# Gate sums with sixteen consecutive tokens in a partition, and gate rows written in 64-byte pieces

## Chip, core and metric

The kernel runs on one core of one Trainium2 chip. The metric is the device time of one execution in microseconds (us). Three runs of the kernel before took 879.82, 880.47 and 882.48 us; the median is 880.47.

The engines are called TensorE (PE in the profile; its weight loads are PEld), VectorE (DVE), ScalarE (ACT), GpSimd (POOL) and SyncE (SP). SBUF is the on-chip memory with 128 partitions, PSUM holds the eight banks into which TensorE accumulates, and DRAM is the memory off the core that only DMAs reach. A DMA is issued by one of the engines, here nearly always SP for loads and POOL for intermediate stores, and is carried out by 16 DMA engines.

## What is computed

The input x has 2048 tokens of 640 features. Two branches read it and a gate mixes them:

```python
x = A_x
g = _sigmoid((x * gate_w).sum(-1, keepdims=True))
a = _A_ref(x, A_dft_seq_re, A_dft_seq_im, A_dft_hid_re, A_dft_hid_im)
b = _B_ref(x, B_w1, B_b1, B_w2)
return g * a + (1 - g) * b
```

Branch A is the real part of a Fourier transform over features and tokens, written as matrix products: `y = Cr @ (x @ Wr^T) - Ci @ (x @ Wi^T)`. Branch B is a dense layer of 1728 units, the Mish activation, and a dense layer back to 640. The gate g is one number for each token: the sigmoid of the sum over features of x times `gate_w`.

## The kernel before

All products are float32 in accuracy, made on TensorE from a high and a low part. For each operand ScalarE rounds the tile to a high part (a tile `r3h` or `w14h`), VectorE subtracts it from the tile to get the low part (`r3l`, `w14l`), and three matmuls (high x high, high x low, low x high) go into the same PSUM bank. There are ten pairs of moving operands r0 to r9 of 128 x 512, so ScalarE and VectorE can run ten operands ahead of TensorE. The larger products use a scheme with seven in place of eight block products, for which VectorE adds and subtracts tiles beforehand (line 259) and adds results afterwards.

Tokens are cut into four groups t of 512. The work runs in this order:

1. Four sequence problems `sq[0]` to `sq[3]` (real and imaginary part, two pairs of token groups each): the sequence DFT matrices against x. Their results u go through DRAM (`u<-f` stores by POOL, `f<-u` loads by SP).
2. Two hidden problems `hd[0]` and `hd[1]` (two token groups each): the hidden DFT matrices against u. Their results are multiplied by g, token by token, and stored as y in DRAM.
3. The first dense layer, with Mish, and for token groups 2 and 3 a product with 1 - g; results go to DRAM as act.
4. Two output problems `ou[0]` and `ou[1]`: the second dense layer, with y added, to the output.

Each of these problems has three parts, `first`, `second` and `third`. The end of `third` reads the PSUM banks out (`done`, `give`, lines 499 to 515); with `self.q` set, as for the hidden problems, the reading is a VectorE product with a tile that holds g of the token group in all 128 partitions. The `second` of the next problem starts accumulating into the same banks.

The order of instructions is decided while the kernel is built. Everything is recorded in a graph of operations with their dependencies, and `Graph.run` (lines 99 to 184) is a list scheduler with a modelled cost for each operation. The order in which it picks operations is the order of each engine's program. The modelled size that it gets for the gates' row writes is a constant, `1 << 18`. Besides waiting for what they read or overwrite, SP's DMAs go round eight semaphores: each waits for the one issued eight earlier to land. A wait at the head of an engine's program holds everything behind it on that engine.

The gate is made by `gates()`, which is recorded between the second and third part of `sq[2]`:

- `gate_w` is loaded into all 128 partitions (`wide`).
- For each k from 0 to 15 a tile of 128 tokens is loaded into an x buffer (line 745), and VectorE multiplies it with `wide` and sums over the features into column k of `gcol`, a tile of 128 x 16 (line 746). In x as the kernel holds it, [16, 128, 640], tile k has tokens 128 k to 128 k + 127, so that `gcol[p, k]` belongs to token 128 k + p.
- ScalarE takes the sigmoid of `gcol` (line 750), VectorE makes `qcol` = 1 - `gcol` (line 751).
- Both are written to DRAM rows `grow` and `qrow` of 2048 numbers in the order of tokens (line 753). In this order element (p, k) goes to place 128 k + p.
- Later, `broadcast` (line 542) loads 512 numbers of a row into all 128 partitions as one tile f. `grow` is used by the hidden problems, `qrow` by the first dense layer and `ou[0]`.

Of the kernel before, what the change touches and what calls it, by code (L numbers as in the profile page):

```python
# [14 lines left out]
S, D, F = 2048, 640, 1728  # L15
P = 128
N = 512
TG = S // N
KS = S // P
# [173 lines left out]
def fnet_mish_gate(ctx: ExitStack, tc: tile.TileContext, xn, xt, c_re, c_im, wd_re, wd_im,  # L193
                   w1a, w1b, b1a, b1b, w2, gw, out):
    nc = tc.nc
# [11 lines left out]
    X = Pool("x", [sb.tile([P, D], F32, name=f"x{i}") for i in range(NX)], FS, lambda t: t[:, :N])  # L207
# [20 lines left out]
    def whole(*vals):  # L228
        return [(v, None) for v in vals]

    def dve(emit, r, w, n=N, more=0.0):
        took = 0.15 + n / 960 + more
        return G.add("DVE", emit, r, w, took, took - 0.083)

    def act(emit, r, w, n=N, more=0.0):
        took = 0.21 + n / 1260 + more
        return G.add("ACT", emit, r, w, took, took - 0.096)

    def dma(queue, emit, r, w, size):
        return G.add(queue, emit, r, w, 1.95 + size / 385e3, 0.605 if queue == "SP" else 1.0)  # L240
# [3 lines left out]
    def load(pool, src, of=None, rows=P, cols=N, queue="SP"):  # L244
        v = Val(pool)
        dma(queue, lambda: ISSUE[queue].dma_start(v.t[:rows, :cols], src() if callable(src) else src),
            whole(of) if of else [], whole(v), rows * cols * 4)
        return v
# [492 lines left out]
    def gates():  # L741

        wide = load(X, gw.partition_broadcast(P), cols=D)
        for k in range(KS):
            x = load(X, xn[k], cols=D)
            dve(lambda k=k, x=x: nc.vector.scalar_tensor_tensor(  # L746
                x.t, x.t, 1.0, wide.t, op0=OP.mult, op1=OP.mult, accum_out=gcol.t[:, k:k + 1]),
                whole(x, wide), whole(x) + [(gcol, k)], D, 0.1)
        cols = [(gcol, k) for k in range(KS)]
        act(lambda: nc.scalar.activation(gcol.t, gcol.t, AF.Sigmoid), cols, cols, KS)  # L750
        dve(lambda: nc.vector.tensor_scalar(qcol.t, gcol.t, -1.0, 1.0, op0=OP.mult, op1=OP.add), cols, whole(qcol), KS)
        for c, row, r in ((gcol, grow, cols), (qcol, qrow, whole(qcol))):
            dma("SP", lambda c=c, row=row: nc.sync.dma_start(row.t.rearrange("o (k p) -> p (o k)", p=P), c.t),
                r, whole(row), 1 << 18)
        act(lambda: nc.scalar.preload_act_table_set("mish"), cols, whole(table), 0, 1.0)

# [29 lines left out]
    for q in range(4):  # L786
        if q == 3:
            sq[3].first(seq_top)
        sq[q].second(seq.low)
        if q == 2:  # L790
            gates()
        sq[q].third()
# [64 lines left out]
```

## Time and profile before

| What | Before |
|---|---|
| Median of three runs | 880.47 us (879.82 to 882.48) |
| Profiled execution, its time | 882.19 us |
| Profiled execution, its span | 880.4 us |
| Instructions | 11973 |
| DMA traffic | 203.50 MB, mean 231 GB/s |
| Mean granted TensorE clock | 0.994 |

The span is the time from the first to the last instruction of the core; the time of the execution has some 1.8 us around it. In the profile a row of a timeline gives the start, the duration in us, the engine, the line of the kernel, the operation and the tiles as `out<-in`, with buffer numbers left out (`f<-u` is any load of a u tile into any f buffer), and in square brackets the idle time of the engine just before and what ended it. A row of waits gives the engine, line and tile that waited, what it waited for, the total in us, how often, and the longest. A row of a table of stretches gives the stretch (start:end in us), its length, and for PE, PEld, DVE, ACT and POOL the busy time with the count of instructions, then the granted TensorE clock, the DMA engines' mean busy share and the GB/s that they moved. A row of DMA issues gives the transfer, the issuing engine, the count, the size, and the median time in us from issue to landing. The chain of waits gives the start, the duration and what the end of the work waited for in that time.

### The profile page before, as it was taken

How to read it: one execution, taken by the hardware profiler on the slowest of the kernel's cores; microseconds unless marked ns; L12 is line 12 of the kernel's file. 1: busy time of each engine (PE TensorE's matmuls, PEld its weight loads, DVE VectorE, ACT ScalarE, POOL GpSimd, SP SyncE). 2: the span in 40 equal slices, each digit the busy share in tenths (PEclk: the TensorE clock that was granted, in tenths of full speed). 3: DMA queues.
4: the chain of work that ended last, by engine and by line, in shares of the span. 5: the costliest groups of instructions: out<-in, count | busy, mean ns of one | idle time of the engine just before them, and what ended most of it. 6: DMA issues, size and time to landing. Idle time of an engine off the chain costs nothing.

```text
span 880.4 us, 11973 instructions
## 1 busy us (share of the span) xinstructions
PE 861.5 (98%) x3772; PEld 710.2 (81%) x3772; DVE 677.8 (77%) x1213; ACT 461.6 (52%) x849; POOL 69.3 (8%) x132
## 2 busy tenths in 40 slices
PE   9999999999999999999995999999999999999998
PEld 7888888888888888888884888888888888887786
DVE  7899957866785667997976999924666997739891
ACT  7675535535453445674552576745655755522541
POOL 0000001002000200011001102111111100000000
PEclk9999999999999999999997999999999999999999
DMA  9796939555954755559975959565444687526943
GB/s 319 273 337 223 324 123 366 181 204 164 346 191 146 254 202 179 196 200 367 374 193 154 373 179 338 211 222 190 146 159 188 214 304 265 199 77 221 366 160 119
DMA packets 107071, 203.50 MB, mean 231 GB/s; under 512 B 16640, under 2 KB 19072, under 8 KB 107008
## 3 DMA queue, kind: packets, MB, share of 16 engines
q1 hardware_dynamic: 96752, 169.57, 56.5%
q0 software_dynamic: 10112, 33.04, 10.0%
q8 instruction: 29, 0.48, 0.2%
q14 instruction: 34, 0.28, 0.1%
q10 hardware_dynamic: 144, 0.13, 0.0%
HBM read 164.40 MB, written 38.29 MB: 230 GB/s over the span
## 4 chain that ended last, share of the span: by engine, by line
PE 85%; DMA 6%; DVE 6%; ACT 1%; issue 1%; SPq 0%; ACTq 0%; DVEq 0%
PE ps L292 85%; DMA f<-u 4%; DVE f L259 3%; DMA x<-in_xn_dram 1%; DMA f<-po 1%; DVE x L746 1%; DVE x L259 0%; DVE r8l L287 0%; ACT f L268 0%; DVE r9l L287 0%; DMA out_dram<-f 0%; ACT r8h L286 0%; DVE r1l L287 0%; DVE r5l L287 0%; ACT r1h L286 0%
## 5 line engine op out<-in xcount | busy, mean ns | idle before, releaser
L259 DVE TENSOR_TENSOR f<-f,f 128x512 f32<-128x512 f32 x316 | 211.8, 686 | 19.6 <-DMA f<-u 15.3
L268 ACT ACTIVATE f<-ps 128x512 f32<-128x512 f32 x129 | 74.5, 595 | 40.2 <-PE ps L292 35.1
L259 DVE TENSOR_TENSOR f<-ps,f 128x512 f32<-128x512 f32 x92 | 59.8, 684 | 38.4 <-PE ps L292 38.3
L255 POOL DMA_DIRECT2D u<-f x40 | 21.5, 540 | 321.6 <-DVE f L259 310.3
L286 ACT ACTIVATE r4h<-f 128x512 fp32r<-128x512 f32 x40 | 25.2, 629 | 37.9 <-PE ps L292 20.2
L286 ACT ACTIVATE r6h<-f 128x512 fp32r<-128x512 f32 x40 | 25.3, 631 | 37.5 <-PE ps L292 17.3
L286 ACT ACTIVATE r1h<-f 128x512 fp32r<-128x512 f32 x39 | 24.5, 629 | 33.0 <-PE ps L292 17.7
L550 ACT ACTIVATE f<-f,b1s 128x512 f32<-128x512 f32 x36 | 25.6, 722 | 28.2 <-DVE f L259 28.1
L286 ACT ACTIVATE r3h<-f 128x512 fp32r<-128x512 f32 x41 | 25.8, 629 | 26.0 <-PE ps L292 13.1
L286 ACT ACTIVATE r2h<-f 128x512 fp32r<-128x512 f32 x41 | 25.8, 628 | 25.4 <-PE ps L292 16.6
L286 ACT ACTIVATE r9h<-f 128x512 fp32r<-128x512 f32 x42 | 26.4, 629 | 23.1 <-PE ps L292 10.7
L255 POOL DMA_DIRECT2D act<-f x52 | 28.2, 542 | 131.0 <-DVE f L259 65.3
L286 ACT ACTIVATE r5h<-f 128x512 fp32r<-128x512 f32 x40 | 25.1, 629 | 25.3 <-PE ps L292 13.3
L287 DVE TENSOR_TENSOR r3l<-f,r3h 128x512 fp32r<-128x512 f32 x41 | 28.2, 688 | 11.6 <-ACT r3h L286 11.2
L286 ACT ACTIVATE r8h<-f 128x512 fp32r<-128x512 f32 x39 | 24.5, 629 | 24.0 <-PE ps L292 14.8
L286 ACT ACTIVATE r0h<-f 128x512 fp32r<-128x512 f32 x40 | 25.1, 629 | 22.1 <-PE ps L292 13.9
L287 DVE TENSOR_TENSOR r9l<-f,r9h 128x512 fp32r<-128x512 f32 x42 | 28.9, 688 | 9.6 <-ACT r9h L286 9.0
L287 DVE TENSOR_TENSOR r0l<-f,r0h 128x512 fp32r<-128x512 f32 x40 | 27.5, 688 | 11.4 <-ACT r0h L286 11.3
L287 DVE TENSOR_TENSOR r2l<-f,r2h 128x512 fp32r<-128x512 f32 x41 | 28.2, 688 | 10.0 <-ACT r2h L286 9.7
L287 DVE TENSOR_TENSOR r8l<-f,r8h 128x512 fp32r<-128x512 f32 x39 | 26.8, 688 | 11.3 <-ACT r8h L286 11.0
L287 DVE TENSOR_TENSOR r6l<-f,r6h 128x512 fp32r<-128x512 f32 x40 | 27.5, 688 | 9.7 <-ACT r6h L286 9.4
L287 DVE TENSOR_TENSOR r5l<-f,r5h 128x512 fp32r<-128x512 f32 x40 | 27.5, 688 | 9.2 <-ACT r5h L286 8.9
(1827 smaller groups left out, 2650.0 us busy)
## 6 DMA issues: line engine op xcount, KB each, us to landing
f<-in_c_re_dram SPq DMA_DIRECT2D x128, 256.0 KB, 4.9
f<-in_c_im_dram SPq DMA_DIRECT2D x128, 256.0 KB, 3.5
f<-act SPq DMA_DIRECT2D x84, 256.0 KB, 5.2
f<-u SPq DMA_DIRECT2D x80, 256.0 KB, 5.7
act<-f POOLq DMA_DIRECT2D x52, 256.0 KB, 2.9
f<-in_xt_dram SPq DMA_DIRECT2D x44, 256.0 KB, 4.4
u<-f POOLq DMA_DIRECT2D x40, 256.0 KB, 5.2
x<-in_xn_dram SPq DMA_DIRECT2D x25, 320.0 KB, 5.7
```

Of the source, the lines that this page charges most:

```text
L255: dma(queue, lambda: ISSUE[queue].dma_start(d.t, v.t[:rows]), whole(v), whole(d), rows * N * 4)
L259: dve(lambda: nc.vector.tensor_tensor(o.t[rows, x], a.t[rows, y], b.t[rows, z], op=op), whole(a, b), whole(o), n)
L268: act(lambda: nc.scalar.activation(o.t, a.t, AF.Copy, scale=scale), whole(a), whole(o))
L286: act(lambda: nc.scalar.activation(r.t[0][:, :N], src.t[:, :N], AF.Copy), whole(src), [(r, 0)])
L287: dve(lambda: nc.vector.tensor_tensor(r.t[1][:, :N], src.t[:, :N], f32(r.t[0][:, :N]), op=OP.subtract), whole(src) + [(r, 0)], [(r, 1)])
L292: G.add("PE", lambda: nc.tensor.matmul(bank.t, w.t[wn][:, k * P:k * P + P], x.t[xn_][:, :N], start, stop, skip_group_check=True), [(w, (k, ...
L550: act(lambda: nc.scalar.activation(o.t[rows], src.t[rows], AF.Mish, **more), whole(src, table) + whole(b1s) * bias, whole(o), more=0.1)
L746: dve(lambda k=k, x=x: nc.vector.scalar_tensor_tensor(x.t, x.t, 1.0, wide.t, op0=OP.mult, op1=OP.mult, accum_out=gcol.t[:, k:k + 1]), whol ...
```

## The change

```diff
     def gates():
 
         wide = load(X, gw.partition_broadcast(P), cols=D)
+        tokens = xn.rearrange("k p d -> (k p) d").rearrange("(p k) d -> k p d", k=KS)
         for k in range(KS):
-            x = load(X, xn[k], cols=D)
+            x = load(X, tokens[k], cols=D)
             dve(lambda k=k, x=x: nc.vector.scalar_tensor_tensor(
                 x.t, x.t, 1.0, wide.t, op0=OP.mult, op1=OP.mult, accum_out=gcol.t[:, k:k + 1]),
                 whole(x, wide), whole(x) + [(gcol, k)], D, 0.1)
...
         for c, row, r in ((gcol, grow, cols), (qcol, qrow, whole(qcol))):
-            dma("SP", lambda c=c, row=row: nc.sync.dma_start(row.t.rearrange("o (k p) -> p (o k)", p=P), c.t),
+            dma("SP", lambda c=c, row=row: nc.sync.dma_start(row.t.rearrange("o (p k) -> p (o k)", k=KS), c.t),
                 r, whole(row), 1 << 18)
```

Tile k of the gate's loads now has the tokens k, 16 + k, 32 + k and so on, one for each partition: a partition's row is still 640 numbers (2560 bytes) in one piece, and the rows of neighbouring partitions are 16 tokens, 40,960 bytes, apart in DRAM, where they were 2560 bytes apart. `gcol[p, k]` then belongs to token 16 p + k, so that the 16 numbers of a partition are 16 neighbours in the row. The row writes, 8 KB each, put each partition's 64 bytes at one place; before, each of the 2048 numbers of 4 bytes went to a place of its own. The contents of `grow` and `qrow` and all that reads them are the same. The sizes, the dependencies and the modelled costs that the scheduler sees are the same as well, and so is the order of each engine's program.

## The prediction

> **What bounds the kernel now.** I read five views in this order: the totals by engine, TensorE's waits over the whole span, the chain of waits from 440 us on, sums of short stretches with the DMA rate, and the timelines of the engines around the one large gap. TensorE is busy nearly all the span, and more than half of what it lacks is a single wait:
>
> ```profile
> PE 861.5 (98%) x3772; PEld 710.2 (81%) x3772; DVE 677.8 (77%) x1213; ACT 461.6 (52%) x849; POOL 69.3 (8%) x132
> ```
> ```profile
> PE ps L292 <- DVE f L259: 10.3, 1, 10.3
> PE ps L292 <- ACT ps L268: 2.2, 3, 1.5
> ```
> ```profile
> 469.91 0.39 PE L292 MATMUL ps<-r3l,w15h 128*128 128x512 f32 x1
> 470.13 0.39 PE L292 MATMUL ps<-r3h,w15l 128*128 128x512 f32 x1
> 480.82 0.76 PE L292 MATMUL ps<-r4h,w11h 128*128 128x512 f32 x1 [10.30 <-DVE f L259]
> ...
> 484.77 0.39 PE L292 MATMUL ps<-r5h,w21h 128*128 128x512 f32 x1
> ```
>
> The pace is one matmul in 0.227 us (469.91 to 470.13, and 133 recorded in 30 us further below). So the matmul at 480.82 was due at 470.36, and the one at 484.77, nine matmuls on, at 470.36 + 9 x 0.227 = 472.40. TensorE has lost 12.4 us by then: 10.46 of standing still, and 1.9 because the nine ran at half clock (the first row of the next fence, granted clock 0.50). This is the seam between the first and second hidden-DFT problem, and the wait is on VectorE reading a PSUM bank that the next problem overwrites. Why is VectorE late? The stretches show the DMA rate, in the last column, almost vanish twice; the last but one is the DMA share:
>
> ```profile
> 474.50:484.70 10.20, 3.88 (x9) 3.13 (x10) 10.02 (x17) 4.62 (x8) 3.40 (x7) 0.50 0.46 160
> ...
> 400.00:430.00 30.00, 30.00 (x133) 24.78 (x132) 25.00 (x50) 13.34 (x25) 2.53 (x5) 1.00 1.04 390
> 430.00:442.00 12.00, 12.00 (x54) 9.95 (x53) 12.00 (x23) 6.66 (x13) 0.00 (x0) 1.00 1.01 371
> 447.00:454.00 7.00, 7.00 (x32) 5.82 (x31) 3.61 (x6) 3.50 (x6) 0.00 (x0) 1.00 0.42 34
> 462.50:469.00 6.50, 6.50 (x30) 5.38 (x29) 1.19 (x2) 0.63 (x1) 0.00 (x0) 1.00 0.46 31
> 445.00:474.50 29.50, 25.52 (x113) 20.82 (x111) 16.56 (x32) 7.92 (x14) 0.00 (x0) 1.00 0.67 143
> ```
> ```profile
> 442.10 0.37 SPq L753 DMA_DIRECT2D grow<-gcol  x1
> ```
> ```profile
> 442.77 12.22 DMA f<-u
> ...
> 457.44 0.37 SPq L753
> ...
> 457.86 13.29 DMA f<-u
> ```
> ```profile
> f<-u SPq DMA_DIRECT2D x80, 256.0 KB, 5.7
> grow<-gcol SPq DMA_DIRECT2D x1, 8.0 KB, 11.9
> qrow<-qcol SPq DMA_DIRECT2D x1, 8.0 KB, 11.1
> ```
>
> Each hole follows one of the two row writes, issued at 442.1 and 457.44. An 8 KB write takes 11.9 and 11.1 us to land, and the 256 KB load issued right behind it 12.2 and 13.3 instead of the usual 5.7. For 7 and 6.5 us the queues hold work (DMA share 0.42 and 0.46) and move 34 and 31 GB/s, where 390 is normal. In the program a row write is 2048 pieces of 4 bytes: consecutive tokens lie in different partitions, so no two elements of a partition are neighbours in the row. VectorE then stands waiting for loads:
>
> ```profile
> 447.43 0.69 DVE L287 TENSOR_TENSOR r7l<-f,r7h 128x512 fp32r<-128x512 f32 x1
> 450.38 0.69 DVE L259 TENSOR_TENSOR f<-f,f 128x512 f32<-128x512 f32 x1 [2.27 <-DMA f<-u]
> ...
> 455.02 0.69 DVE L259 TENSOR_TENSOR f<-f,f 128x512 f32<-128x512 f32 x1 [2.14 <-DMA f<-u]
> ...
> 467.81 0.69 DVE L259 TENSOR_TENSOR f<-f,f 128x512 f32<-128x512 f32 x1 [7.07 <-DMA f<-u]
> ...
> 471.24 0.69 DVE L259 TENSOR_TENSOR f<-f,f 128x512 f32<-128x512 f32 x1 [1.47 <-DMA f<-u]
> ...
> 476.40 3.08 DVE L259 TENSOR_TENSOR f<-ps,f 128x512 f32<-128x512 f32 x5
> ...
> 479.99 1.28 DVE L259 TENSOR_TENSOR f<-ps,f 128x512 f32<-128x512 f32 x2
> ...
> 483.59 1.28 DVE L259 TENSOR_TENSOR f<-ps,f 128x512 f32<-128x512 f32 x2
> 484.79 0.68 DVE L287 TENSOR_TENSOR r9l<-f,r9h 128x512 fp32r<-128x512 f32 x1
> ```
>
> The four waits are 12.95 us. The bank reads at 476.40 to 483.59 stand behind them in VectorE's order, and the first of the pair at 479.99 frees the bank that TensorE waits for.
>
> **The change, part by part.** The order of instructions on every engine is the same in both kernels, so no queue is reshuffled and no instruction added. Three things differ.
>
> *The row writes.* Each becomes 128 pieces of 64 bytes, one for each partition, in place of 2048. No small write to DRAM other than these two stands in this trace. Bounds of a landing: the ordinary 5.7 us of a load in a full queue (or the 4.6 of a store, below) from one side, the 11.9 of today from the other. If the holes go with the number of pieces, 7 and 6.5 us become 7/16 = 0.44 and 6.5/16 = 0.41; if with the bytes, nothing changes. I take the first: the DMA engines had the same work queued in the holes as before them, and ordinary stores, with 32 times the bytes in long pieces, land in 4.6 us.
>
> The Trainium skill (DMA: Bandwidth & Descriptors, Specifications) speaks against half of this: a transfer below 512 bytes costs a read-modify-write, and 64 is still below. If each piece pays, the holes shrink by 16 as above; if being small were enough to stop the queue, the time would stay.
>
> *What becomes of the stall.* VectorE from 448.1 to 484.79 has 36.7 - 12.95 = 23.7 us of work, so without waits it could start r9l at 471.8. Its bank reads must also wait for TensorE. By the program's order the last 30 matmuls before the seam are 18 for one group of banks and 12 for the last pair, so the banks come free at 470.36 - 30 x 0.227 = 463.6, at 467.6 and at 470.4. VectorE would reach the five reads of 476.40 at 476.4 - 12.95 = 463.5, just when the first banks are done; the read that releases TensorE (479.99, now 467.0 at the earliest) waits for 467.6 and ends by 468.3, 2 us before TensorE needs it at 470.36. The last pair starts at 470.4, so r9l starts at about 471.8, 13 us earlier than 484.79. TensorE thus loses neither the 10.46 nor the 1.9 us.
>
> Can the DMAs keep up? From 445 to 474.5 they moved 29.5 us x 143 GB/s = 4.2 MB; at 385 GB/s that is 11 us, so it can be in by 456 to 460 even where SP issues late. The next loads hang on the stores of y, which follow the products with g:
>
> ```profile
> 480.04 1.60 POOL L255 DMA_DIRECT2D y<-f  x3 [58.42 <-DVE f L259]
> ```
> ```profile
> 483.30 20.59 SPq L246 DMA_DIRECT2D f<-u  x25
> ```
> ```profile
> y<-f POOLq DMA_DIRECT2D x20, 256.0 KB, 4.6
> x<-in_xn_dram SPq DMA_DIRECT2D x25, 320.0 KB, 5.7
> ```
>
> The first store waits for a product after the five bank reads: 463.6 + 5 x 0.6 + 0.6 = 467.2 in place of 480.04, so the 25 loads that begin at 483.30 begin 12 to 13 us earlier too. The whole pipeline moves, not TensorE alone. That matters, because VectorE is then full for long, and TensorE gets an operand only just in time:
>
> ```profile
> 496.00:575.00 79.00, 79.00 (x350) 65.45 (x349) 78.75 (x156) 54.72 (x112) 10.87 (x20) 1.00 0.74 261
> ```
> ```profile
> 552.12 0.68 DVE L287 TENSOR_TENSOR r5l<-f,r5h 128x512 fp32r<-128x512 f32 x1
> ```
> ```profile
> 553.72 0.39 PE L292 MATMUL ps<-r5l,w17h 128*128 128x512 f32 x1
> ```
>
> VectorE is busy 78.75 of 79 us here, and r5l is ready at 552.80, 0.9 us before use. If VectorE came only 10 us earlier, TensorE would stall 12.4 - 10 - 0.9 = 1.5 us.
>
> *The token loads.* The 16 loads of x for the gates take rows 16 apart, a pitch of 40,960 bytes instead of 2560, still 128 pieces of 2560 bytes. They lie in 400 to 442 us, where the DMAs are full, but TensorE has a cushion there:
>
> ```profile
> 423.42 0.68 DVE L287 TENSOR_TENSOR r3l<-f,r3h 128x512 fp32r<-128x512 f32 x1
> ```
> ```profile
> 433.87 0.39 PE L292 MATMUL ps<-r3l,w0h 128*128 128x512 f32 x1
> ```
>
> r3l waits 433.87 - 424.10 = 9.8 us for its use. No load with this pitch stands in the trace. Bounds: no extra, or each 320 KB (0.84 us at 390 GB/s) at half speed, 16 x 0.84 = 13.4 us, of which the cushion takes 9.8 and 3.6 us would show. I take nothing, since the pieces keep their size.
>
> The Trainium skill (DMA: Bandwidth & Descriptors, Latency and other measured facts) lists copies that lose from a 2 MiB row pitch on, and full speed at 512 KiB; 40 KiB is far below, and by it the sum stays. No run shows it yet.
>
> **Sum.** 10.46 + 1.9 = 12.4 us off the profiled execution's 882.19 us (880.4 of span and 1.8 around it) is 869.8. That execution lies 1.7 above the median of 880.47. If the 1.7 lies elsewhere the changed median is 868.1; if the stall itself varies between runs it goes with it, and 869.8 holds for all. I take 868.9, a gain of 11.6.
>
> **The rivals.**
> - *The write stalls whatever its pieces.* For it: only these two small writes exist, so pieces and bytes cannot be told apart here. Against it: 8 KB is a thirty-second of an ordinary store. Time: 880.5.
> - *The holes only halve, or VectorE moves less than TensorE.* Holes of 3.5 and 3.25 us give VectorE 6.75 us back; 10.46 - 6.75 = 3.7 us of gap stay, and too short a gap to lose the clock (it fell at 474.5, 4.1 us after TensorE stopped). Gain 12.4 - 3.7 = 8.7, time 871.8. The tight stretch with a late VectorE (1.5 us, above) gives about 870.4.
> - *Slower: the wide pitch starves the full DMA queue.* With e us more for each token load, TensorE loses 16e - 9.8, and the kernel ends slower once 16e exceeds 9.8 + 12.4 - 0.8 = 21.4, so from e = 1.34 us, a load at 38% of today's speed. At e = 2 the time is 868.9 + 32 - 9.8 = 891. For it: DMA share 1.04 in 400 to 430, nothing to spare. Against: pieces of 2560 bytes as before.
>
> **Chances.** The forecast (stall gone, 867 to 870.3) 0.72; partly gone or partly given back (870.3 to 877) 0.15; the write stalls as before 0.06; slower by the pitch 0.07. A measurement of this kernel can tell about 0.3%, 2.6 us, from no change. Faster 0.87, same 0.06, slower 0.07. The range takes the whole recovery from the fastest run shown (879.82 - 12.4 = 867.4, and 0.5 below it) to the halved holes with 1 us over: 866.9 to 872.8.
>
> **What would show it.** Row writes landing in 3 to 6 us; no stretch of several us below 50 GB/s with loads queued; VectorE's 7.07 us wait gone; TensorE's wait of 10.3 us gone or under 1 us, its clock at 1.00 across the seam; the stores of y beginning near 467. Token loads should land as the 5.7 us of today. Wrong would be: writes that still take 10 us, a TensorE wait for operands between 520 and 560 of over 2 us, or VectorE waiting on token loads before 445.

## The result and the profile after

| What | Before | After |
|---|---|---|
| Median | 881.22 us (879.82 to 882.48, 4 runs) | 869.34 us (869.13 to 870.01, 4 runs) |
| Ratio of after to before, 95% interval | | 0.9867 (0.9849 to 0.9885) |
| Profiled execution, its time | 882.19 us | 869.13 us |
| Profiled execution, its span | 880.4 us | 867.3 us |
| Mean granted TensorE clock | 0.994 | 1.00 |

One run of the kernel before was added to the three shown at first, which moves its median from 880.47 to 881.22. The changed kernel is 1.3% faster, 11.9 us; the interval is clear of 1.

The totals of the changed kernel, and all of TensorE's waits in it:

```profile
PE 859.1 (99%) x3772; PEld 708.8 (82%) x3772; DVE 677.4 (78%) x1213; ACT 462.6 (53%) x849; POOL 69.4 (8%) x132
```
```profile
PE ps L715 <- DVE r9l L713: 2.0, 1, 2.0
PE ps L292 <- ACT ps L268: 1.6, 3, 1.0
PE ps L292 <- ACT r1h L286: 0.4, 1, 0.4
PE ps L292 <- DVE r1l L287: 0.3, 1, 0.3
```

The wait of 10.3 us on VectorE is not there any more, and nothing has taken its place. The longest left is the 2.0 us before the first matmul. VectorE's work is the same (677.8 us before, 677.4 after): time was saved by when it is done, not by how much there is.

TensorE at the seam between the two hidden problems, from its timeline. The last matmul of the first problem and the first of the second are one pace apart:

```profile
469.74 0.39 PE L292 MATMUL ps<-r3h,w15l 128*128 128x512 f32 x1
469.97 0.39 PE L292 MATMUL ps<-r4h,w11h 128*128 128x512 f32 x1
...
472.01 0.39 PE L292 MATMUL ps<-r5h,w21h 128*128 128x512 f32 x1
```

The matmul that started at 484.77 before starts at 472.01, 12.76 us earlier. Of this, 0.39 us is from before the seam (the last matmul before it is at 469.74, not at 470.13). The seam itself gives 12.37 us: the standing still and the half clock.

The two row writes among the DMA issues (size, us from issue to landing), the three stretches of the two holes and of the half clock, with the DMA share and GB/s in the last two columns, and the stretch in which grow lands now (it is issued at 440.47, qrow at 451.79):

```profile
grow<-gcol SPq DMA_DIRECT2D x1, 8.0 KB, 5.0
qrow<-qcol SPq DMA_DIRECT2D x1, 8.0 KB, 1.4
```
```profile
447.00:454.00 7.00, 7.00 (x33) 5.79 (x32) 7.00 (x14) 3.04 (x6) 0.00 (x0) 1.00 0.63 193
462.50:469.00 6.50, 6.50 (x30) 5.41 (x29) 6.50 (x12) 3.03 (x6) 2.14 (x4) 1.00 0.49 163
474.50:484.70 10.20, 10.20 (x46) 8.45 (x45) 8.31 (x15) 3.88 (x7) 0.00 (x0) 1.00 1.04 382
```
```profile
440.50:445.50 5.00, 5.00 (x24) 4.14 (x23) 5.00 (x9) 4.97 (x9) 0.00 (x0) 1.00 1.05 390
```

While grow lands, the loads go on at 390 GB/s, so its hole is gone. Where 34 and 31 GB/s moved, 193 and 163 do now, and VectorE is busy for 7.00 of 7.00 and 6.50 of 6.50 us where it was busy for 3.61 and 1.19; these two stretches lie behind the landings now. The stretch of half clock (474.5 to 484.7) is at full clock. VectorE's timeline shows the bank reads no longer late:

```profile
446.36 0.69 DVE L287 TENSOR_TENSOR r7l<-f,r7h 128x512 fp32r<-128x512 f32 x1
446.97 0.69 DVE L259 TENSOR_TENSOR f<-f,f 128x512 f32<-128x512 f32 x1
...
455.01 0.69 DVE L259 TENSOR_TENSOR f<-f,f 128x512 f32<-128x512 f32 x1
...
462.66 3.08 DVE L259 TENSOR_TENSOR f<-ps,f 128x512 f32<-128x512 f32 x5
...
466.25 1.28 DVE L259 TENSOR_TENSOR f<-ps,f 128x512 f32<-128x512 f32 x2
...
469.85 1.28 DVE L259 TENSOR_TENSOR f<-ps,f 128x512 f32<-128x512 f32 x2
471.05 0.68 DVE L287 TENSOR_TENSOR r9l<-f,r9h 128x512 fp32r<-128x512 f32 x1
```

The instructions at 446.97 and 455.01 are those that started at 450.38 and 467.81 before, with 2.27 and 7.07 us of waiting in front; now each follows the instruction before it. What came behind moved along: the first store of y to 466.30 (480.04 before), the long run of loads to 469.55 (483.30 before).

```profile
466.30 1.60 POOL L255 DMA_DIRECT2D y<-f  x3 [45.65 <-DVE f L259]
```
```profile
469.55 20.53 SPq L246 DMA_DIRECT2D f<-u  x25
```

### The profile page after: what moved, and what is told of

Its sections match the earlier page's. It is cut to its first block, busy times and chain, and to the rows that moved or that the text cites. A ratio compares the mean times of both kernels' runs of the same rounds, so it can differ in the third digit from the quotient of the medians.

```text
span 867.3 us, 11973 instructions
## 1 busy us (share of the span) xinstructions
PE 859.1 (99%) x3772; PEld 708.8 (82%) x3772; DVE 677.4 (78%) x1213; ACT 462.6 (53%) x849; POOL 69.4 (8%) x132
## 4 chain that ended last, share of the span: by engine, by line
PE 96%; DMA 2%; DVE 2%; ACT 0%; issue 0%; SPq 0%; ACTq 0%; DVEq 0%
PE ps L292 95%; DVE f L259 1%; DMA out_dram<-f 1%; DMA f<-act 1%; PE ps L715 0%; DVE x L259 0%; DVE r1l L287 0%; ACT r3h L286 0%; ACT r4h L286 0%; DVE r3l L287 0%; ACT f L268 0%; ACT r5h L286 0%; SPq L246 0%; ACT ps L268 0%; DVE r9l L713 0%
## 5 line engine op out<-in xcount | busy, mean ns | idle before, releaser
L286 ACT ACTIVATE r9h<-f 128x512 fp32r<-128x512 f32 x42 | 26.4, 629 | 23.3 <-PE ps L292 11.4
L287 DVE TENSOR_TENSOR r3l<-f,r3h 128x512 fp32r<-128x512 f32 x41 | 28.2, 689 | 11.4 <-ACT r3h L286 11.1
L287 DVE TENSOR_TENSOR r8l<-f,r8h 128x512 fp32r<-128x512 f32 x39 | 26.9, 690 | 13.1 <-ACT r8h L286 12.8
L286 ACT ACTIVATE r7h<-f 128x512 fp32r<-128x512 f32 x39 | 24.6, 631 | 19.9 <-PE ps L292 13.3
```

Of the source, the lines that this page charges most:

```text
L286: act(lambda: nc.scalar.activation(r.t[0][:, :N], src.t[:, :N], AF.Copy), whole(src), [(r, 0)])
L287: dve(lambda: nc.vector.tensor_tensor(r.t[1][:, :N], src.t[:, :N], f32(r.t[0][:, :N]), op=OP.subtract), whole(src) + [(r, 0)], [(r, 1)])
```

## The experiments

Three questions: does the gain come from the writes alone; how does it depend on the pieces; and what about the pieces makes the holes. The runs were made on several chips. Each group has its own runs of the kernel before beside it, whose medians are 882.42, 884.75 and 883.87 us, so across groups the ratios are to be compared, not the times.

### One half of the change at a time

Only the row writes changed:

```diff
-            dma("SP", lambda c=c, row=row: nc.sync.dma_start(row.t.rearrange("o (k p) -> p (o k)", p=P), c.t),
+            dma("SP", lambda c=c, row=row: nc.sync.dma_start(row.t.rearrange("o (p k) -> p (o k)", k=KS), c.t),
```

> Only the row writes are changed (64-byte pieces); the token loads stay contiguous, so that the gates belong to other tokens and the output is not the reference's. Theory (the pieces of the row writes make the holes): the whole gain is here, 868.5 to 870.5 us, row writes landing in under 6 us, TensorE's wait at the seam gone. Rival (the new pitch of the token loads contributes): more than 1 us above the changed kernel's 869.3 or below 868.

Measured: 869.64 us (868.89 to 869.94), ratio 0.9848 (0.9826 to 0.9871), landings 5.0 and 1.4 us, no wait on VectorE at the seam. The whole gain is in the writes.

Only the token loads changed:

```diff
+        tokens = xn.rearrange("k p d -> (k p) d").rearrange("(p k) d -> k p d", k=KS)
         for k in range(KS):
-            x = load(X, xn[k], cols=D)
+            x = load(X, tokens[k], cols=D)
```

> Only the token loads are changed (rows 40,960 bytes apart); the row writes stay in 2048 pieces of 4 bytes, so that the gates belong to other tokens and the output is not the reference's. Theory: no change, 879.5 to 882.5 us, row writes landing in 11 to 12 us, TensorE's wait at the seam 9 to 11 us, median landing of the token loads 5.5 to 6.2 us. Rival (the pitch costs, hidden in the cushion): landings over 7 us, or more than 883 us.

Measured: 882.85 us, beside 882.42 of before, ratio 1.0000 (0.9984 to 1.0015); the median lies 0.35 us above the expected range and 0.43 above that of before. The 16 token loads land in 5.8 us in the median, 5.9 before. TensorE's longest wait and the row writes, from the views of waits and DMA issues of this run:

```profile
PE ps L292 <- DVE f L259: 10.6, 1, 10.6
```
```profile
grow<-gcol SPq DMA_DIRECT2D x1, 8.0 KB, 12.2
qrow<-qcol SPq DMA_DIRECT2D x1, 8.0 KB, 11.1
```

The wider pitch costs nothing, and is not merely hidden: the loads themselves are no slower. The stall is as it was.

One write alone back in 4-byte pieces, in the changed kernel (here grow; for the other run qrow):

```diff
+            view = "o (k p) -> p (o k)" if row is grow else "o (p k) -> p (o k)"
-            dma("SP", lambda c=c, row=row: nc.sync.dma_start(row.t.rearrange("o (p k) -> p (o k)", k=KS), c.t),
+            dma("SP", lambda c=c, row=row, view=view: nc.sync.dma_start(row.t.rearrange(view, p=P), c.t),
```

> The changed kernel, but grow alone is again written in 4-byte pieces (its g then stands in another order of tokens, so the output is not the reference's). In the changed kernel VectorE frees the bank 3.1 us before TensorE needs it. The first hole made VectorE wait 4.4 us, so TensorE should stand about 1.3 us: 870 to 871.5 us. Rival (each write gives half of the gain): 874 to 876 us.

> The changed kernel, but qrow alone is again written in 4-byte pieces (its 1 - g then stands in another order of tokens, so the output is not the reference's). VectorE's waits of 7.07 and 1.47 us come back, less the 3.1 us of room: TensorE stands 5 to 6 us at the seam and loses 0.5 to 1.9 us to its clock, 875 to 877.5 us. Rival (each write gives half of the gain): 874 to 876 us with a gap of 4 us. Rival (the holes only hurt together): under 871 us.

Measured: with grow in small pieces 876.42 us, ratio 0.9904 (0.9887 to 0.9922), with qrow 878.90, ratio 0.9936 (0.9919 to 0.9953). TensorE at the seam, first with grow, then with qrow: the last matmul of the first problem, the first of the second, and the one nine matmuls on.

```profile
471.02 0.39 PE L292 MATMUL ps<-r3h,w15l 128*128 128x512 f32 x1
475.33 0.77 PE L292 MATMUL ps<-r4h,w11h 128*128 128x512 f32 x1 [3.92 <-DVE f L259]
...
479.06 0.40 PE L292 MATMUL ps<-r5h,w21h 128*128 128x512 f32 x1
```
```profile
470.87 0.39 PE L292 MATMUL ps<-r3h,w15l 128*128 128x512 f32 x1
477.00 0.77 PE L292 MATMUL ps<-r4h,w11h 128*128 128x512 f32 x1 [5.74 <-DVE f L259]
...
480.98 0.63 PE L292 MATMUL ps<-r5h,w21h 128*128 128x512 f32 x1
```

The 5.7 us is as worked out (5 to 6). The 3.9 is three times the 1.3 expected for grow: in front of the seam that run's VectorE waited 6.5 us for loads (1.41, 4.85 and 0.27), not 4.4. The two long ones:

```profile
450.53 0.69 DVE L259 TENSOR_TENSOR f<-f,f 128x512 f32<-128x512 f32 x1 [1.41 <-DMA f<-u]
...
457.88 0.69 DVE L259 TENSOR_TENSOR f<-f,f 128x512 f32<-128x512 f32 x1 [4.85 <-DMA f<-u]
```

What the expectation left out is SP: the load of g for the broadcast stands in SP's program until grow has landed, 13.1 us after its issue here, and every later load stands behind it. In this run's chain of waits, that landing (13.12 us) and a load issued behind it (6.20) stand in front of VectorE's work at 463.87.

Both times lie above the expected ones. With grow the gap is larger, and the clock, which was not counted, comes on top. Nine matmuls at full pace take 2.04 us; here they take 3.73 and 3.98, and from 474 to 485 us the granted clock is 0.84 and 0.69 on average. So a gap of 3.9 us was already long enough to lose the clock. With grow TensorE loses 4.1 us of standing and 1.7 of clock, 5.8 in all; with qrow 5.9 and 1.9, and 0.6 more in the next three matmuls, 8.4 in all. Over the 869.13 us of the profiled execution of the changed kernel, 1.5 and 0.8 us are left; no kernel without small pieces ran on this chip, so the runs don't say what they are. The two losses are not parts of the 12.4 us of both: each run has the 3 us of room for itself and pays for a fall of the clock.

### Larger pieces

Each partition holds groups of b neighbouring tokens, b = 2 or 4, and the loads match:

```diff
+        tokens = xn.rearrange("k p d -> (k p) d").rearrange("(a p b) d -> a b p d", p=P, b=2)
-            x = load(X, xn[k], cols=D)
+            x = load(X, tokens[k // 2, k % 2], cols=D)
...
-            ... nc.sync.dma_start(row.t.rearrange("o (k p) -> p (o k)", p=P), c.t)
+            ... nc.sync.dma_start(row.t.rearrange("o (a p b) -> p (o a) b", p=P, b=2),
+                                  c.t.rearrange("p (a b) -> p a b", b=2))
```

> Rows written in 1024 pieces of 8 bytes, the token loads laid out to match. Theory A (a hole goes with the number of pieces): holes of about 3.5 us each, VectorE gets 6.75 us back, TensorE stands 3.7 us at the seam and keeps its clock, 872 to 874 us. Theory B (the hole goes with the bytes, or with pieces that fill less than 64 bytes): as before, 879.5 to 882.5 us.

> Rows written in 512 pieces of 16 bytes, the token loads laid out to match. Theory A (number of pieces): holes of about 1.7 us each, VectorE gets 10 us back, TensorE stands less than 1 us at the seam, 869 to 870.5 us. Theory B (bytes, or pieces under 64 bytes): as before, 879.5 to 882.5 us.

Measured: 871.09 us with 8 bytes, ratio 0.9868 (0.9847 to 0.9888), and 869.74 with 16, ratio 0.9848 (0.9829 to 0.9868). In neither does TensorE wait for VectorE at the seam; the 872 to 874 expected for 8 bytes is missed on the low side. The row writes, first with 8, then with 16 bytes, and the one wait for loads of VectorE in front of the seam with 8 bytes:

```profile
grow<-gcol SPq DMA_DIRECT2D x1, 8.0 KB, 6.4
qrow<-qcol SPq DMA_DIRECT2D x1, 8.0 KB, 5.3
```
```profile
grow<-gcol SPq DMA_DIRECT2D x1, 8.0 KB, 5.2
qrow<-qcol SPq DMA_DIRECT2D x1, 8.0 KB, 2.9
```
```profile
457.86 0.69 DVE L259 TENSOR_TENSOR f<-f,f 128x512 f32<-128x512 f32 x1 [1.30 <-DMA f<-u]
```

For qrow the landing is 11.1, 5.3, 2.9 and 1.4 us with 2048, 1024, 512 and 128 pieces, close to proportional down to a floor. What VectorE loses falls faster: with half the pieces it waits 1.30 us in front of the seam (0.42 with 16 bytes), where 12.95 - 6.75 = 6.2 had been expected. SP's timeline shows one reason. In the kernel before, the instruction that issues the load behind grow itself takes 3.80 us:

```profile
442.77 3.80 SPq L246 DMA_DIRECT2D f<-u  x1
```

With 8, 16 and 64 bytes it takes the usual 0.32. So behind grow, 2048 pieces also hold up SP itself, and 1024 no longer do. Behind qrow alone, in the run above, three such issues take 1.89 us together, so more than the number plays a part. The bytes are always 8 KB, so theory B falls. But a piece twice as long also shares its 64 bytes with half as many others, and the next runs part the two.

### What about the pieces

Now the changed kernel keeps its 64-byte writes and gets one extra write behind each, which nothing reads. Only the extra one's pattern differs:

```diff
+            extra = Val(t=dr.tile([1, S * e], F32, ...))
+            dma("SP", lambda ...: nc.sync.dma_start(extra.t.rearrange("o (k p e) -> p (o k) e", p=P, e=e)[:, :, :1], ...),
+                r, whole(extra), 1 << 18)
```

The dense run has e = 1, the sparse one e = 16; the two with pieces 8 bytes apart have e = 2, with `(k p e)` for neighbours from different partitions and `(p k e)` for neighbours from one; the control writes 64-byte pieces.

> The changed kernel with one more write behind each row write, which nothing reads, in 64-byte pieces: the control for the runs with extra writes. All theories: an extra write in itself costs nothing, ratio to the kernel before 0.984 to 0.989, no gap at the seam, landings under 6 us.

> The changed kernel with one more write behind each row write, which nothing reads: the same 2048 numbers in 4-byte pieces, neighbouring addresses coming from neighbouring partitions as before the change. Both theories: landing 10 to 12 us, the holes and most of the stall are back, 877 to 882 us. It is the yardstick for the next one.

> As the run with the extra dense write, but the 4-byte pieces of the extra write stand 64 bytes apart (a scratch row of 128 KB). Theory A (the number of pieces counts): landing 10 to 12 us and the time of the dense one within 1 us. Theory C (pieces that share 64 bytes with pieces from other partitions block each other): landing under 5 us and 869 to 871.5 us.

> The extra writes in 2048 pieces of 4 bytes, 8 bytes apart, a partition's 16 pieces side by side: eight pieces share 64 bytes and come from one partition. Theory C (pieces from different partitions in the same 64 bytes block each other): like the sparse run, landing 5 to 7.5 us, ratio 0.984 to 0.990. Theory D (pieces in the same 64 bytes block each other, whoever sends them): landing 9 to 13 us, ratio 0.994 to 1.002.

> The same addresses as in the run before, 8 bytes apart, but neighbours come from neighbouring partitions: eight pieces share 64 bytes and come from eight partitions. Theories C and D: landing 9 to 13 us, ratio 0.994 to 1.002. If neither sharing counts but the spread of the addresses over 16 KB: landing 7 to 9 us, the same as the run before.

| Extra write, 8 KB | Pieces in 64 bytes, from | Landing of the two, us | TensorE's wait at the seam, us | Ratio to before (95%) |
|---|---|---|---|---|
| 128 pieces of 64 bytes | 1 | 4.3, 1.5 | none | 0.9837 (0.9822 to 0.9852) |
| 2048 of 4, 64 bytes apart | 1 | 6.6, 6.7 | 1.8 | 0.9858 (0.9837 to 0.9880) |
| 2048 of 4, 8 bytes apart | 8, eight partitions | 8.2, 9.4 | 4.0 | 0.9912 (0.9888 to 0.9935) |
| 2048 of 4, dense | 16, sixteen partitions | 11.4, 13.2 | 12.7 | 1.0000 (0.9989 to 1.0011) |
| 2048 of 4, 8 bytes apart | 8, one partition | 17.0, 15.3 | 17.2 | 1.0037 (1.0022 to 1.0052) |

The DMA issues of the three most telling ones, in this order: the control, the sparse run, and the run with eight pieces from one partition.

```profile
extrag<-gcol SPq DMA_DIRECT2D x1, 8.0 KB, 4.3
...
extraq<-qcol SPq DMA_DIRECT2D x1, 8.0 KB, 1.5
```
```profile
extrag<-gcol SPq DMA_DIRECT2D x1, 8.0 KB, 6.6
...
extraq<-qcol SPq DMA_DIRECT2D x1, 8.0 KB, 6.7
```
```profile
extrag<-gcol SPq DMA_DIRECT2D x1, 8.0 KB, 17.0
...
extraq<-qcol SPq DMA_DIRECT2D x1, 8.0 KB, 15.3
```

The control costs nothing, so it is not the extra DMA as such that costs here. The dense run brings the whole stall back though nothing reads its extra writes; its 884.83 us lie above the 877 to 882 expected. Its chain of waits runs through two slow loads (start, us):

```profile
445.11 15.04 DMA f<-u
460.16 13.63 DMA f<-u
```

All four others issue the same number of equally small pieces, and their landings reach from 6.6 to 17.0 us. So the number of pieces alone (theory A) doesn't set the cost: where they land counts too. The number still counts for something. With pieces 64 bytes apart the loads get 98 GB/s from 448 to 454 us, TensorE waits 1.8 us, and the landings are above the 5 us of theory C. The issue of the load behind the first extra write is held up whatever the pattern, for 3.04 to 3.24 us in the four runs; here the sparse run and the control:

```profile
446.15 3.04 SPq L246 DMA_DIRECT2D f<-u  x1
```
```profile
445.66 0.32 SPq L246 DMA_DIRECT2D f<-u  x1
```

Theory C falls hardest in the run with eight pieces from one partition: it expected 5 to 7.5 us where a partition has its 64 bytes to itself, and that is the slowest pattern of all, above the ratio that either theory gave it. Theory D, that pieces in the same 64 bytes hold each other up whoever sends them, has the signs right (both patterns with sharing are slower than the sparse one) but not the sizes: it expected 9 to 13 us for both runs 8 bytes apart, and they are 8.2 to 9.4 and 15.3 to 17.0. In the slowest pattern the pieces of the same 64 bytes also follow each other in the order of the write, partition by partition. That neighbours close in time are the worst fits all five rows; it is a reading of them, and no run tested it by itself. The landings are those of writes among other work: qrow's own 64-byte write, issued right ahead of the extra one, lands in 12.1 us in the dense run and 16.5 in the slowest, where it takes 1.4 in the changed kernel. In the slowest run SP adds to the gap: its second extra write, the eighth DMA behind the first, is issued only when the first has landed, at 462.62, and the later loads stand behind it. During its first landing the stretch from 449 to 460 us of that run moves 28 GB/s:

```profile
449.00:460.00 11.00, 11.00 (x51) 9.09 (x50) 8.67 (x16) 3.58 (x7) 0.00 (x0) 1.00 0.63 28
```

### Another queue

The kernel before, with its 4-byte row writes issued by ScalarE's queue:

```diff
-            dma("SP", lambda c=c, row=row: nc.sync.dma_start(row.t.rearrange("o (k p) -> p (o k)", p=P), c.t),
-                r, whole(row), 1 << 18)
+            G.add("ACT", lambda c=c, row=row: nc.scalar.dma_start(row.t.rearrange("o (k p) -> p (o k)", p=P), c.t),
+                  r, whole(row), 2.6, 0.1)
```

> The kernel before, its two row writes in 4-byte pieces issued by ScalarE's queue instead of SyncE's (the scheduler then moves a few instructions of ScalarE and renames buffers). Theory M (the holes arise where the pieces are written, so that every queue suffers): ratio 0.995 to 1.005, TensorE's gap at the seam 8 to 12 us. Theory Q (the loads are stuck behind the pieces in SyncE's own queue): loads go on at over 150 GB/s while the rows land, gap under 3 us, ratio 0.984 to 0.990.

Measured: 878.62 us (876.98 to 884.20), ratio 0.9942 (0.9924 to 0.9961). The profiled execution is the slowest of the ten, at 884.20 us; its row writes, its wait at the seam, and two stretches while grow landed:

```profile
grow<-gcol ACTq DMA_DIRECT2D x1, 8.0 KB, 14.8
qrow<-qcol ACTq DMA_DIRECT2D x1, 8.0 KB, 18.9
```
```profile
PE ps L292 <- DVE f L259: 11.0, 1, 11.0
```
```profile
445.00:452.00 7.00, 7.00 (x33) 5.79 (x32) 4.36 (x8) 6.24 (x10) 0.00 (x0) 1.00 1.17 113
452.00:462.00 10.00, 10.00 (x46) 8.28 (x45) 6.25 (x11) 0.30 (x2) 0.00 (x0) 1.00 0.42 97
```

These rates don't decide between the theories. From 445.0 to 457.9 us SP issues nothing: it stands at the load of g until grow has landed. What decides is how long the loads take that were issued right behind the two writes (grow at 443.07, qrow at 461.32). SP's wait, and the two loads as the chain of waits shows them:

```profile
SPq L246 <- DMA grow<-gcol: 12.8, 1, 12.8
```
```profile
443.36 11.77 DMA f<-u
...
462.94 12.29 DMA f<-u
```

They take 11.8 and 12.3 us, from SP's queue, while the pieces are in ScalarE's; before, with both in one queue, such loads took 12.2 and 13.3. So theory Q falls, and the gap of 11.0 us is within the 8 to 12 of theory M. The 0.6% that the median gains lies just outside what theory M expected. One thing does depend on the queue: the issue of the load at 443.36 takes 0.32 us, not 3.80. Whether the 0.6% comes from that or from the order of instructions, which is a little different in this run, is not shown; the one trace is of the slowest execution. Another queue gives 0.6% where larger pieces give 1.3 to 1.5%.

## Why the prediction was right

*What bounds the kernel.* The one wait at the seam and the half clock behind it were priced at 12.4 us; the seam gave 12.37. The rest of the 13.1 us by which the spans differ lies elsewhere: 0.39 us before the seam, and 0.3 net after it, where the waits that are left in both kernels came out a little different (the waits on ScalarE's bank copies are 2.2 us before and 1.6 after).

*The row writes.* That the holes are made by small pieces was right, and the runs with one half of the change show that nothing else takes part. The first landing, 5.0 us, is within the 3 to 6 forecast; the second, 1.4, is below it: by then the DMA queues are nearly empty (DMA share 0.08 from 451.8 to 453.2 us), and the bounds had been taken from landings in full ones. The step from 2048 to 128 pieces was priced as pieces alone (a hole of 0.44 us). That rule is too simple, as the extra writes and the run with 8 bytes show (TensorE did not wait there, where 3.7 us would follow from it). That it gave the right end here is in part luck: 64-byte pieces have neither the number nor the neighbours.

The Trainium skill (DMA: Bandwidth & Descriptors, Specifications) puts the limit below which a transfer pays a read-modify-write at 512 bytes. No run here has row pieces of 512 bytes or more, so none can show that step. Far below it, two more writes in 64-byte pieces cost nothing that TensorE or the time shows (0.9837 of before), and 16-byte pieces give 0.9848, the same as the writes of 64 bytes alone. Being small was not enough to stop the queue.

*What becomes of the stall.* VectorE arrived as worked out. The five reads begin at 462.66 (forecast 463.6), the pair that frees TensorE's bank at 466.25 (467.6), r9l at 471.05 (471.8), all within 1.4 us and on the early side. VectorE was 1.07 us ahead already at r7l (446.36, 447.43 before), in front of all the waits that went, and TensorE 0.39; neither is in the forecast. One step was wrong without harm: the pair's first read was to wait for TensorE until 467.6, and it started at 466.25 without a wait. The 467.6 is when the last bank of its group is done; each operand's products go bank by bank, three matmuls each, so the first of the three banks is done six matmuls, 1.4 us, earlier. The bank that TensorE needs at 469.97 is free at 466.25 + 0.68 = 466.93, 3 us ahead; 2 had been forecast.

*The tight stretch later.* It did not bite, because VectorE moved 484.79 - 471.05 = 13.7 us while TensorE moved 12.8 at the seam. The forecast had 13 and 12.4. The low part r5l is ready at 538.30 + 0.69 = 538.99, 1.9 us before its use at 540.91, where it was 0.9 us.

*The token loads.* Taken at nothing, and the run with them alone confirms it: ratio 1.0000 and the same landings.

*The sum.* 868.9 was the middle between 869.8 (the profiled execution less 12.4) and 868.1 (the median less 12.4); measured 869.34. The middle was a compromise, and that it lies within 0.5 us of the measured time owes something to luck. The runs since speak for the first reading, that the stall itself varies: the kernel before ran between 879.76 and 887.38 us over all runs here, the changed kernel and the control between 869.13 and 870.18.

*The rivals.* The write that stalls whatever its pieces fell with the runs of 8 and 16 bytes. The half-cured stall comes nearest to what one write alone does, with gaps of 3.9 and 5.7 us where it had 3.7. Its 871.8 us would still have been too low (876.42 and 878.90), in part because it took such a gap as too short to lose the clock, and after 3.9 us TensorE lost it. The slow token loads did not come.

## What to carry to other kernels

Look at the layout of small writes to DRAM as at a cost of everybody's: 8 KB in 4-byte pieces held up 256 KB loads for 7 us, from ScalarE's queue as from SP's, and TensorE stood still 28 us after the first write was issued, at a place that names only VectorE. Lay out the producer, here which tokens a partition gets, so that a partition's numbers are neighbours in the destination; 16 bytes in a piece were already enough here. Before counting on the whole gain, ask whether the engines behind the stall move by as much as the stalled one, and whether they have slack further on.

## What was not expected

Of the patterns with 2048 pieces of 4 bytes, the slowest is not the one whose neighbours come from sixteen partitions (11.4 and 13.2 us) but the one in which a partition writes its own neighbourhood in steps of 8 bytes (17.0 and 15.3), while the same number of pieces 64 bytes apart lands in 6.6 and 6.7. Why is open: the runs don't tell whether it is the 64 bytes, a larger unit, or the order in time that counts. Also, with the small pieces in ScalarE's queue the loads right behind them still took 11.8 and 12.3 us, and the rows themselves landed later, after 14.8 and 18.9 us.
